# Key columns projected from rows without the shift, shift matmuls inside the first projection pass, and softmax read from PSUM, in an adaLN attention block on one core

## The chip, the cores and the metric

The kernel runs on one core of one Trainium2 chip. The metric is device time in microseconds of one execution. Executions are repeated, and each run is listed with its span in the trace and its mean granted TensorE clock. A run is put down as slow when it is over 1.5% above the fastest run of the same kernel; otherwise it is fast. Times of spans, windows and chains below are from the start of the traced span, which is some 1.8 us shorter than the measured time. In the views PE is TensorE, PEld its weight loads, DVE VectorE, ACT ScalarE and SPq the queue that issues transfers; psbank is a PSUM bank, PEclk the granted clock in tenths of full speed, and x with a number counts instructions. A "chain" is the work that ended last, followed back step by step to what released it.

## The reference

Shortened:

```python
B, N, D = (2, 256, 1152)          # bf16 everywhere
mod = (silu(c) @ w_mod).reshape(B, 6, 1, D)
shift_a, scale_a, gate_a, _, _, _ = [mod[:, i] for i in range(6)]
h   = layernorm(x) * (1 + scale_a) + shift_a
q, k, v = split(h @ wqkv)
p = softmax(einsum('bqd,bkd->bqk', q, k) * D ** -0.5)
return x + gate_a * (einsum('bqk,bkd->bqd', p, v) @ wo)
```

One fact of the arithmetic carries the change. If the key columns are made from h without the shift, every key of a batch element lacks the same vector (shift times the key weights). Its product with a query is the same number for all keys, so the softmax over keys cancels it. Queries and values still need the shift.

## The kernel before

All rows are 128-partition tiles: four token tiles, nine feature chunks. A small helper records operations in program order, and each engine is given its own in that order, with semaphore waits for dependences. The parts that matter, shortened:

```python
GROUPS = [(0, 2), (2, 5), (5, 7), (7, 9)]            # feature chunks modulated together
PASSES = [list(range(0, 7)), list(range(7, 14)), list(range(14, 18))]   # q,k column blocks
PASS1_BANKS = [5, 6, 0, 1, 2, 3, 4]
...
def warm(n):                                          # matmuls of zeros that keep TensorE busy
    for _ in range(n):
        op(PE, lambda pe: pe.matmul(ps[7][:, 0:512], warm_sb[:, 0:P], warm_sb[:, 0:512], ...))
...
xT(0); warm(3); xT(1); warm(2)                        # transposes of normalised rows
mod_mm(0, 1); xT_out(0, ...); mod_mm(0, 0); mod_ev(0) # scale and shift of group 0
...
for g, (a, b_) in enumerate(GROUPS):                  # pass 0, in four groups
    if g > 0:
        mod_mm(g, 1); mod_mm(g, 0)                    # scale and shift of this group
        mod_ev(g)                                     # PSUM -> SBUF on DVE
        for cc in range(a, b_):
            for b in range(B):
                modulate(cc, b, ...)                  # hT = xnT * scale + shift
    for k in range(a, b_):
        for j, bank in zip(PASSES[0], PASS1_BANKS):
            qk_mm(0, j, k, bank)
for n, (j, bank) in enumerate(zip(PASSES[0], PASS1_BANKS)):
    evac(DVE if n % 2 == 0 else AC, qkT_sb[:, j, :], ps[bank][:, 0:T], ...)
...                                                   # passes 1 and 2, then v, scores, softmax
```

Softmax copies the scores from PSUM to SBUF on ACT, takes scaled values and their maximum on DVE, then does the exponential on ACT. The weights arrive on one queue, modulation columns and first-pass rows alternating by group.

Of the kernel before, what the change touches and what calls it, by code (L numbers as in the profile page):

```python
# [153 lines left out]
GROUPS = [(0, 2), (2, 5), (5, 7), (7, 9)]  # L154
PASSES = [list(range(0, 7)), list(range(7, 14)), list(range(14, 18))]
# [17 lines left out]
def _build(nc, es, x, c, wqkv, wo, w_mod, out):  # L173
# [19 lines left out]
    s_sb = sb("s_sb", [P, TT, NTOK], bf16)  # L193
# [34 lines left out]
    wm_off = {}  # L228
    off = 0
    for g, (a, b_) in enumerate(GROUPS):  # L230
        for kind in range(2):
            wm_off[(g, kind)] = off
            off += DC * (b_ - a) * P

    def wm_ap(g, kind):
        w = (GROUPS[g][1] - GROUPS[g][0]) * P
        return bass.AP(wm_sb, wm_off[(g, kind)], [[2 * DC * D, P], [w, DC], [1, w]])
# [3 lines left out]

    def wm_keys(lo, hi):
        keys = []
        for (g, kind), o in wm_off.items():
            n = DC * (GROUPS[g][1] - GROUPS[g][0]) * P
            if o < hi and o + n > lo:
                keys.append(("wm", g, kind))
        return keys
# [6 lines left out]
    def dma_mod(g):  # L255
        a, b_ = GROUPS[g]
        for kind in (1, 0):
            base = kind * D
            op(SP, lambda e, g=g, kind=kind, lo=base + a * P, hi=base + b_ * P:
               e.dma_start(wm_ap(g, kind), wm_v[:, :, lo:hi]), w=[("wm", g, kind)], dma=True)  # L260

    def dma_wq(k0, k1, c0, c1, keys):
        op(SP, lambda e: e.dma_start(wq_sb[:, k0:k1, c0:c1], wq_v[:, k0:k1, c0:c1]),
           w=keys, dma=True)

    def wkeys(p, k0, k1):
        return [("w", p, k) for k in range(k0, k1)]

    for g, (a, b_) in enumerate(GROUPS):
        dma_mod(g)  # L270
        dma_wq(a, b_, 0, 7 * P, wkeys(0, a, b_))
    for k0 in range(0, DC, 3):
        dma_wq(k0, k0 + 3, 7 * P, 14 * P, wkeys(1, k0, k0 + 3))
    for k0 in range(0, DC, 3):
        dma_wq(k0, k0 + 3, 14 * P, 18 * P, wkeys(2, k0, k0 + 3))
    for k0 in range(0, DC, 3):
        dma_wq(k0, k0 + 3, 2 * D, 3 * D, wkeys(3, k0, k0 + 3))
# [17 lines left out]
    def warm(n):  # L295
        for _ in range(n):
            op(PE, lambda pe: pe.matmul(ps[7][:, 0:512], warm_sb[:, 0:P], warm_sb[:, 0:512],  # L297
                                        start=True, stop=True),
               r=[("warm",)], w=[("ps", 7)])
# [5 lines left out]
    def f_cT(pe):  # L305
        last = None
        for k in range(DC):
            last = pe.transpose(psb[6][:, 2 * k:2 * k + 2], c_sb[0:2, k * P:(k + 1) * P],
                                ident[0:2, 0:2])
        return last  # L310
    op(PE, f_cT, r=[("c",), ("ident",)], w=[("ps", 6)])
    cT_ps = psb[6][:, 0:2 * DC].rearrange("p (k b) -> p k b", b=2)
    op(DVE, lambda v: v.tensor_copy(cT_sb[:, :, :], cT_ps), r=[("ps", 6)], w=[("cT",)])
    op(AC, lambda a: a.activation(e1_sb[:, :, :], cT_sb[:, :, :], ACT.Exp, scale=-1.0),
       r=[("cT",)], w=[("e1",)])
    warm(8)

# [68 lines left out]
    def mod_mm(g, kind):  # L386
        a, b_ = GROUPS[g]
        w = (b_ - a) * P
        for cc in range(a, b_):
            col = (kind * DC + cc) * 2  # L390
            for k in range(DC):
                op(PE, lambda pe, cc=cc, k=k, col=col, src=wm_ap(g, kind), lo=(cc - a) * P: pe.matmul(  # L392
                    ps[7][:, col:col + 2], src[:, k, lo:lo + P], scT_sb[:, k, 0:2],
                    start=(k == 0), stop=(k == DC - 1)),
                   r=[("wm", g, kind), ("scT",)], w=[("ps", 7)])
# [3 lines left out]
    def mod_ev(g):  # L399
        a, b_ = GROUPS[g]  # L400
        op(DVE, lambda v: v.tensor_scalar(mod_sb[:, 1, a:b_, :], mod_ps[:, 1, a:b_, :], 1.0, None,  # L401
                                          op0=ALU.add), r=[("ps", 7)], w=[("sc", g)])
        op(DVE, lambda v: v.tensor_copy(mod_sb[:, 0, a:b_, :], mod_ps[:, 0, a:b_, :]),  # L403
           r=[("ps", 7)], w=[("sh", g)])

    group_of = {cc: g for g, (a, b_) in enumerate(GROUPS) for cc in range(a, b_)}

    def modulate(cc, b, eng):
        g = group_of[cc]
        dst = hT_sb[:, cc, b * NTOK:(b + 1) * NTOK]  # L410
        src = xnT_sb[:, cc, b * NTOK:(b + 1) * NTOK]
        sc, sh = mod_sb[:, 1, cc, b:b + 1], mod_sb[:, 0, cc, b:b + 1]
        rk, wk = [("xnT", cc, b), ("sc", g), ("sh", g)], [("hT", cc, b)]
        if eng == DVE:
            op(DVE, lambda v: v.tensor_scalar(dst, src, sc, sh, op0=ALU.mult, op1=ALU.add), r=rk, w=wk)  # L415
        else:
            op(AC, lambda a: a.activation(dst, src, ACT.Identity, bias=sh, scale=sc), r=rk, w=wk)  # L417

    stats_dve(0)
# [6 lines left out]
    rstd(0)  # L426
    sq_act(1)
    stats_dve(2)
    stats_act_end(1)
    xn(0)  # L430
    rstd(1)
    rstd(2)
    xn(1)
    xn(2)
    sum_act(3)
    sq_act(3)
    xT(0)
    warm(3)
    xT(1)
    warm(2)  # L440
    mod_mm(0, 1)
    xT_out(0, lambda bank: DVE)
    mod_mm(0, 0)
    mod_ev(0)
    modulate(0, 0, DVE)
    modulate(1, 0, DVE)
    stats_act_end(3)
    rstd(3)
    xn(3)
    xT(2)  # L450
    xT(3)
    xT_out(1, lambda bank: DVE if bank % 2 == 0 else AC)
    modulate(0, 1, DVE)
# [216 lines left out]
```

## Time and profile before

| | before |
|---|---|
| median of the first three runs | 112.39 us (111.78 to 112.62) |
| span of the profiled run | 110.1 us |
| TensorE busy | 99.1 us, 90% |
| first matmul of pass 0 | 16.19 us |
| pass 0, first to last of 63 matmuls | 23.9 us |
| one undisturbed 512-column matmul | 0.219 us |

The prediction shows the slices and the chain. One more view is worth knowing, the table of waits (engine, what it was to make, what it waited for: us in total, times, longest). TensorE's own waits for other engines' work in pass 0 are one line of it:

```profile
PE psbank L459 <- DVE hT_sb L415: 3.5, 4, 1.0
```

These are the four group starts: the projection (L459) waits for the modulated rows (L415). The three inside pass 0 make 2.9 us.

### The profile page before, as it was taken

To read this page: it belongs to the slowest core of one execution; us is meant where nothing else is said; L and a number is where in the kernel's file an instruction comes from. 1 tells how busy PE (TensorE), PEld (TensorE's weight loads), DVE (VectorE), ACT (ScalarE), POOL (GpSimd) and SP (SyncE) were. 2 spreads that over 40 slices of the span, in tenths; PEclk is the share of its full clock that TensorE was granted. 3 is DMA by queue.
4 is the path that set the end of the run, shared out by engine and by line. 5 is a ranking of instruction groups with operands and counts; after the bars stand their busy time and mean duration, and the time that the engine had idled before them with its cause. 6 is when DMAs were issued, how large, how long until landed. Compare 5 with 4: busy or idle time off the path is not lost.

```text
span 110.1 us, 1775 instructions
## 1 busy us (share of the span) xinstructions
PE 99.1 (90%) x735; PEld 56.2 (51%) x735; DVE 43.9 (40%) x125; ACT 26.7 (24%) x61; POOL 4.2 (4%) x17
## 2 busy tenths in 40 slices
PE   5959459969969699999999999999999999999990
PEld 1407333533445334444444568766666875655570
DVE  0798570040030380000800422643422785666672
ACT  4579230030020250000500415461111870000000
POOL 6610000000000000000000000000000000000000
PEclk9999955785999999999999999999999999999999
DMA  3999999999999999996299400000000001112222
GB/s 77 323 309 321 333 332 348 292 329 294 369 382 363 366 390 389 396 392 232 20 361 408 176 0 0 6 3 0 0 0 0 6 0 33 56 54 70 71 77 71
DMA packets 18956, 21.06 MB, mean 191 GB/s; under 512 B 770, under 2 KB 14978, under 8 KB 18948
## 3 DMA queue, kind: packets, MB, share of 16 engines
q1 hardware_dynamic: 18944, 20.94, 58.7%
q8 instruction: 6, 0.10, 0.4%
q14 instruction: 2, 0.02, 0.1%
q10 hardware_dynamic: 4, 0.00, 0.0%
HBM read 19.76 MB, written 1.18 MB: 190 GB/s over the span
## 4 chain that ended last, share of the span: by engine, by line
PE 81%; DMA 7%; DVE 6%; SPq 2%; issue 1%; ACT 0%
PE psbank L459 36%; PE psbank L509 16%; PE psbank L620 16%; DMA wm_sb<-in_w_mod_dram 7%; PE psbank L585 4%; PE psbank L522 4%; PE psbank L392 3%; DVE hT_sb L415 2%; SPq L253 2%; PE psbank L572 1%; DVE xnT_sb L381 1%; PE psbank L601 1%; DVE mod_sb L401 1%; DVE ga_sb L627 1%; DVE xo_sb L362 1%
## 5 line engine op out<-in xcount | busy, mean ns | idle before, releaser
L459 PE MATMUL psbank<-hT_sb,wq_sb 128*128 128x512 bf16 x162 | 39.6, 408 | 3.5 <-DVE hT_sb L415 3.5
L459 PEld LDWEIGHTS psbank<-hT_sb,wq_sb 128*128 128x128 bf16 x162 | 16.3, 104 | 25.4 <-issue 5.1
L509 PE MATMUL psbank<-wq_sb,hT_sb 128*128 128x384 bf16 x108 | 18.0, 326 | 0.0
L620 PE MATMUL psbank<-wm_sb,pvT_sb 128*128 128x384 bf16 (+2 forms) x117 | 17.7, 314 | 0.0
L620 PEld LDWEIGHTS psbank<-wm_sb,pvT_sb 128*128 128x128 bf16 x117 | 11.1, 98 | 6.6
L509 PEld LDWEIGHTS psbank<-wq_sb,hT_sb 128*128 128x128 bf16 x108 | 10.5, 98 | 6.9
L466 DVE CAST qkT_sb<-psbank 128x512 bf16<-128x512 f32 x10 | 6.3, 684 | 18.9 <-PE psbank L459 18.9
L468 ACT ACTIVATE qkT_sb<-psbank 128x512 bf16<-128x512 f32 x8 | 4.2, 597 | 21.2 <-PE psbank L459 21.2
L627 DVE TENSOR_TENSOR ga_sb<-psbank,gate_rep 128x384 bf16<-128x384 f32 (+2 forms) x13 | 6.8, 526 | 5.9 <-PE psbank L620 5.9
L297 PE MATMUL psbank<-warm_sb 128*128 128x512 bf16 x17 | 6.9, 556 | 1.2 <-DVE warm_sb L280 1.2
L401 DVE TENSOR_SCALAR mod_sb<-psbank 128x4 f32<-128x4 f32 (+1 forms) x4 | 0.7, 164 | 17.7 <-PE psbank L392 17.7
L417 ACT ACTIVATE hT_sb<-xnT_sb,mod_sb 128x256 bf16<-128x256 bf16 x4 | 2.3, 596 | 18.6 <-DVE mod_sb L403 18.6
L466 DVE CAST v_sb<-psbank 128x384 bf16<-128x384 f32 x6 | 3.2, 555 | 7.7 <-PE psbank L509 7.7
L369 PE MATMUL psbank<-ident,xo_sb 128*128 128x128 bf16 x36 | 3.1, 242 | 3.4 <-DVE xo_sb L362 3.4
L468 ACT ACTIVATE v_sb<-psbank 128x384 bf16<-128x384 f32 x6 | 2.9, 486 | 10.3 <-PE psbank L509 10.3
L392 PEld LDWEIGHTS psbank<-scT_sb,wm_sb 128*128 128x128 bf16 x162 | 4.7, 96 | 1.3 <-DMA wm_sb<-in_w_mod_dram 0.3
L392 PE MATMUL psbank<-scT_sb,wm_sb 128*128 128x2 bf16 x162 | 4.8, 164 | 0.2 <-DMA wm_sb<-in_w_mod_dram 0.2
L369 PEld LDWEIGHTS psbank<-ident,xo_sb 128*128 128x128 bf16 x36 | 2.5, 108 | 4.7 <-DVE xo_sb L362 4.5
L630 DVE TENSOR_TENSOR xo_sb<-x_sb,ga_sb 128x384 bf16<-128x384 bf16 (+2 forms) x13 | 4.5, 342 | 0.4
L585 PE MATMUL psbank<-pT_sb,v_sb 128*128 128x256 bf16 x36 | 4.3, 273 | 0.0
L522 PE MATMUL psbank<-qkT_sb 128*128 128x256 bf16 x36 | 4.1, 273 | 0.0
L415 DVE TENSOR_SCALAR hT_sb<-xnT_sb,mod_sb 128x256 bf16<-128x256 bf16 x14 | 4.0, 342 | 0.1
(57 smaller groups left out, 59.0 us busy)
## 6 DMA issues: line engine op xcount, KB each, us to landing
wm_sb<-in_w_mod_dram SPq DMA_DIRECT2D x6, 576.0 KB, 8.3
wq_sb<-in_wqkv_dram SPq DMA_DIRECT2D x4, 672.0 KB, 8.6
wq_sb<-in_wqkv_dram SPq DMA_DIRECT2D x3, 864.0 KB, 11.1
wm_sb<-in_w_mod_dram SPq DMA_DIRECT2D x1, 2592.0 KB, 17.8
wm_sb<-in_wo_dram SPq DMA_DIRECT2D x1, 2592.0 KB, 9.2
wm_sb<-in_w_mod_dram SPq DMA_DIRECT2D x2, 864.0 KB, 8.9
wq_sb<-in_wqkv_dram SPq DMA_DIRECT2D x3, 448.0 KB, 8.3
x_sb<-in_x_dram SPq DMA_DIRECT2D x4, 288.0 KB, 3.6
```

What stands on the lines that cost most here:

```text
L297: op(PE, lambda pe: pe.matmul(ps[7][:, 0:512], warm_sb[:, 0:P], warm_sb[:, 0:512], start=True, stop=True), r=[("warm",)], w=[("ps", 7)])
L369: op(PE, lambda pe, cc=cc, bank=bank, half=half: pe.transpose(psb[bank][:, half * T + i * P: half * T + (i + 1) * P], xo_sb[:, i, cc * P:( ...
L392: op(PE, lambda pe, cc=cc, k=k, col=col, src=wm_ap(g, kind), lo=(cc - a) * P: pe.matmul(ps[7][:, col:col + 2], src[:, k, lo:lo + P], scT_s ...
L415: op(DVE, lambda v: v.tensor_scalar(dst, src, sc, sh, op0=ALU.mult, op1=ALU.add), r=rk, w=wk)
L459: op(PE, lambda pe: pe.matmul(ps[bank][:, lo:hi], wq_sb[:, k, j * P:(j + 1) * P], hT_sb[:, k, lo:hi], start=(k == 0), stop=(k == DC - 1)), ...
L466: op(DVE, lambda v: v.tensor_copy(dst, src), r=r, w=w)
L468: op(AC, lambda a: a.activation(dst, src, ACT.Copy), r=r, w=w)
L509: op(PE, lambda pe, k=k, q=q, bank=bank: pe.matmul(ps[bank][:, 0:384], hT_sb[:, k, i * P:(i + 1) * P], wq_sb[:, k, 2 * D + q * 384:2 * D + ...
L522: op(PE, lambda pe, cc=cc: pe.matmul(ps[bank][:, 0:NTOK], qkT_sb[:, cc, i * P:(i + 1) * P], qkT_sb[:, DC + cc, b * NTOK:(b + 1) * NTOK], s ...
L585: op(PE, lambda pe, h=h, cc=cc, sbk=sbk: pe.matmul(ps[bank][:, h * NTOK:(h + 1) * NTOK], v_sb[:, 2 * b + sbk, cc * P:(cc + 1) * P], pT_sb[ ...
L620: op(PE, lambda pe, i=i, k=k, c0=c0, c1=c1, n=n, bank=bank: pe.matmul(ps[bank][:, 0:n], pvT_sb[:, k, i * P:(i + 1) * P], wo_ap[:, k, c0:c1 ...
L627: op(DVE, lambda v, b=b, c0=c0, c1=c1, n=n, bank=bank, s=s: v.tensor_tensor(ga_sb[:, s, 0:n], ps[bank][:, 0:n], gate_rep[:, b, c0:c1], ALU ...
```

## The change

The intent is to take everything that TensorE waits for out of pass 0. The columns are reordered so that pass 0 makes key columns alone (blocks 11 to 17), from rows that are only scaled. The scale half of the modulation is made before pass 0, row by row as it arrives. The shift half is made by matmuls between those of pass 0, added to the rows after it, and used by passes 1 and 2 and by v. Weights come in longer rows. Softmax reads its scores from PSUM. The activation table set is not changed by the diff, and both profiles have one table load, of 1.28 us. The diff also reorders the row statistics on ACT and shares the evictions of the transposes between DVE and ACT in another way. No run takes these two, or the longer rows, out on their own.

```diff
-PASSES = [list(range(0, 7)), list(range(7, 14)), list(range(14, 18))]
+PASSES = [list(range(11, 18)), list(range(4, 11)), list(range(0, 4))]
@@ loads
-    for g, (a, b_) in enumerate(GROUPS):
-        dma_mod(g)
-        dma_wq(a, b_, 0, 7 * P, wkeys(0, a, b_))
+    for k0 in range(0, DC, 3):
+        dma_mod(1, k0, k0 + 3)                 # scale half, whole rows
+    dma_pass(0, [0, 1, 3, 6, 9])
+    for k0 in range(0, DC, 3):
+        dma_mod(0, k0, k0 + 3)                 # shift half
@@ before pass 0 (cut; the first burst of warm-ups goes from 8 to 6)
     xT(0)
-    warm(3)
+    for k in range(0, 3):
+        mod_mm(1, k)
+    warm(2)
     xT(1)
     warm(2)
...
     xT(2)
+    for k in range(3, 6):
+        mod_mm(1, k)
+    warm(3)
     xT(3)
     xT_out(1, ...)
+    warm(2)
+    for k in range(6, 9):
+        mod_mm(1, k)
+    op(DVE, ...)                               # 1 + scale, then scale(cc, b) for all rows
@@ pass 0
-    for g, (a, b_) in enumerate(GROUPS):
-        ...                                    # as shown above
+    for k in range(DC):
+        for j, bank in zip(PASSES[0], PASS1_BANKS):
+            qk_mm(0, j, k, bank)
+        if 5 <= k <= 7:
+            for kk in range(3 * (k - 5), 3 * (k - 4)):
+                mod_mm(0, kk)
+    op(DVE, lambda v: v.tensor_copy(mod_sb[:, 0, :, :], mod_ps[:, 0, :, :]), ...)
+    for cc in range(DC - 1):
+        for b in range(B):
+            shift(cc, b, DVE if (2 * cc + b) % 3 else AC)
     for n, (j, bank) in enumerate(zip(PASSES[0], PASS1_BANKS)):
         evac(DVE if n % 2 == 0 else AC, qkT_sb[:, j, :], ps[bank][:, 0:T], ...)
+    for b in range(B):
+        shift(DC - 1, b, DVE)
@@ softmax (cut)
-        op(AC, lambda a: a.activation(s_sb[:, i, :], ps[bank][:, 0:NTOK], ACT.Copy), ...)
-        op(DVE, ... s_sb * CONST_B, max into mx_sb ...)
+        op(DVE, lambda v: v.tensor_reduce(mx_sb[:, i:i + 1], ps[bank][:, 0:NTOK], AX.X, ALU.max), ...)
```

More of the change, by code (lines that the diff above doesn't have):

```diff
@@ L152 @@
 CONST_B = 0.0294189453125
-GROUPS = [(0, 2), (2, 5), (5, 7), (7, 9)]
-PASSES = [list(range(0, 7)), list(range(7, 14)), list(range(14, 18))]
+PASSES = [list(range(11, 18)), list(range(4, 11)), list(range(0, 4))]
 PASS1_BANKS = [5, 6, 0, 1, 2, 3, 4]
@@ L192, in _build @@
     wm_sb = sb("wm_sb", [P, 2 * DC * D], bf16)
-    s_sb = sb("s_sb", [P, TT, NTOK], bf16)
     e_sb = sb("e_sb", [P, TT, NTOK], bf16)
@@ L226, in _build, with wm_ap @@
     op = pg.op
-    wm_off = {}
-    off = 0
-    for g, (a, b_) in enumerate(GROUPS):
-        for kind in range(2):
-            wm_off[(g, kind)] = off
-            off += DC * (b_ - a) * P
-    def wm_ap(g, kind):
-        w = (GROUPS[g][1] - GROUPS[g][0]) * P
-        return bass.AP(wm_sb, wm_off[(g, kind)], [[2 * DC * D, P], [w, DC], [1, w]])
+    def wm_ap(kind):
+        return bass.AP(wm_sb, kind * DC * D, [[2 * DC * D, P], [D, DC], [1, D]])
     wgate_ap = bass.AP(wm_sb, 0, [[2 * DC * D, P], [D, DC], [1, D]])
     wo_ap = bass.AP(wm_sb, DC * D, [[2 * DC * D, P], [D, DC], [1, D]])
-    def wm_keys(lo, hi):
-        keys = []
-        for (g, kind), o in wm_off.items():
-            n = DC * (GROUPS[g][1] - GROUPS[g][0]) * P
-            if o < hi and o + n > lo:
-                keys.append(("wm", g, kind))
-        return keys
     op(AC, lambda e: e.dma_start(c_sb[:, :], c[:, :]), w=[("c",)], dma=True)
@@ L253, in _build, with dma_mod, dma_wq, dma_pass @@
         op(SP, lambda e, i=i: e.dma_start(x_sb[:, i, :], x_pi[:, i, :]), w=[("x", i)], dma=True)
-    def dma_mod(g):
-        a, b_ = GROUPS[g]
-        for kind in (1, 0):
-            base = kind * D
-            op(SP, lambda e, g=g, kind=kind, lo=base + a * P, hi=base + b_ * P:
-               e.dma_start(wm_ap(g, kind), wm_v[:, :, lo:hi]), w=[("wm", g, kind)], dma=True)
-    def dma_wq(k0, k1, c0, c1, keys):
-        op(SP, lambda e: e.dma_start(wq_sb[:, k0:k1, c0:c1], wq_v[:, k0:k1, c0:c1]),
-           w=keys, dma=True)
-    def wkeys(p, k0, k1):
-        return [("w", p, k) for k in range(k0, k1)]
-    for g, (a, b_) in enumerate(GROUPS):
-        dma_mod(g)
-        dma_wq(a, b_, 0, 7 * P, wkeys(0, a, b_))
+    def dma_mod(kind, k0, k1):
+        op(SP, lambda e: e.dma_start(wm_ap(kind)[:, k0:k1, :], wm_v[:, k0:k1, kind * D:(kind + 1) * D]),
+           w=[("wm", kind, k) for k in range(k0, k1)], dma=True)
+    def dma_wq(p, k0, k1, c0, c1):
+        op(SP, lambda e: e.dma_start(wq_sb[:, k0:k1, c0:c1], wq_v[:, k0:k1, c0:c1]),
+           w=[("w", p, k) for k in range(k0, k1)], dma=True)
+    def dma_pass(p, cuts):
+        c0, c1 = PASSES[p][0] * P, (PASSES[p][-1] + 1) * P
+        for k0, k1 in zip(cuts, cuts[1:]):
+            dma_wq(p, k0, k1, c0, c1)
     for k0 in range(0, DC, 3):
-        dma_wq(k0, k0 + 3, 7 * P, 14 * P, wkeys(1, k0, k0 + 3))
+        dma_mod(1, k0, k0 + 3)
+    dma_pass(0, [0, 1, 3, 6, 9])
     for k0 in range(0, DC, 3):
-        dma_wq(k0, k0 + 3, 14 * P, 18 * P, wkeys(2, k0, k0 + 3))
+        dma_mod(0, k0, k0 + 3)
+    dma_pass(1, [0, 3, 6, 9])
+    dma_pass(2, [0, 3, 6, 9])
     for k0 in range(0, DC, 3):
-        dma_wq(k0, k0 + 3, 2 * D, 3 * D, wkeys(3, k0, k0 + 3))
+        dma_wq(3, k0, k0 + 3, 2 * D, 3 * D)
     op(DVE, lambda v: v.memset(warm_sb[:, :], 0.0), w=[("warm",)])
@@ L296, in warm @@
         for _ in range(n):
-            op(PE, lambda pe: pe.matmul(ps[7][:, 0:512], warm_sb[:, 0:P], warm_sb[:, 0:512],
+            op(PE, lambda pe: pe.matmul(ps[6][:, 0:512], warm_sb[:, 0:P], warm_sb[:, 0:512],
                                         start=True, stop=True),
-               r=[("warm",)], w=[("ps", 7)])
+               r=[("warm",)], w=[("ps", 6)])
     op(AC, lambda a: a.preload_act_table_set("natural_log_exp_and_others"))
@@ L307, in f_cT @@
         for k in range(DC):
-            last = pe.transpose(psb[6][:, 2 * k:2 * k + 2], c_sb[0:2, k * P:(k + 1) * P],
+            last = pe.transpose(psb[5][:, 2 * k:2 * k + 2], c_sb[0:2, k * P:(k + 1) * P],
                                 ident[0:2, 0:2])
         return last
-    op(PE, f_cT, r=[("c",), ("ident",)], w=[("ps", 6)])
-    cT_ps = psb[6][:, 0:2 * DC].rearrange("p (k b) -> p k b", b=2)
-    op(DVE, lambda v: v.tensor_copy(cT_sb[:, :, :], cT_ps), r=[("ps", 6)], w=[("cT",)])
+    op(PE, f_cT, r=[("c",), ("ident",)], w=[("ps", 5)])
+    cT_ps = psb[5][:, 0:2 * DC].rearrange("p (k b) -> p k b", b=2)
+    op(DVE, lambda v: v.tensor_copy(cT_sb[:, :, :], cT_ps), r=[("ps", 5)], w=[("cT",)])
     op(AC, lambda a: a.activation(e1_sb[:, :, :], cT_sb[:, :, :], ACT.Exp, scale=-1.0),
        r=[("cT",)], w=[("e1",)])
-    warm(8)
     def stats_dve(i):
@@ L384, in xT_out, with mod_mm @@
                    r=[("ps", bank)], w=keys)
-    def mod_mm(g, kind):
-        a, b_ = GROUPS[g]
-        w = (b_ - a) * P
-        for cc in range(a, b_):
+    def mod_mm(kind, k):
+        for cc in range(DC):
             col = (kind * DC + cc) * 2
-            for k in range(DC):
-                op(PE, lambda pe, cc=cc, k=k, col=col, src=wm_ap(g, kind), lo=(cc - a) * P: pe.matmul(
-                    ps[7][:, col:col + 2], src[:, k, lo:lo + P], scT_sb[:, k, 0:2],
-                    start=(k == 0), stop=(k == DC - 1)),
-                   r=[("wm", g, kind), ("scT",)], w=[("ps", 7)])
@@ L397, in _build @@
-    mod_ps = ps[7][:, 0:4 * DC].rearrange("p (q c b) -> p q c b", q=2, b=2)
-    def mod_ev(g):
-        a, b_ = GROUPS[g]
-        op(DVE, lambda v: v.tensor_scalar(mod_sb[:, 1, a:b_, :], mod_ps[:, 1, a:b_, :], 1.0, None,
-                                          op0=ALU.add), r=[("ps", 7)], w=[("sc", g)])
-        op(DVE, lambda v: v.tensor_copy(mod_sb[:, 0, a:b_, :], mod_ps[:, 0, a:b_, :]),
-           r=[("ps", 7)], w=[("sh", g)])
-    group_of = {cc: g for g, (a, b_) in enumerate(GROUPS) for cc in range(a, b_)}
@@ L408, in modulate, with scale @@
-    def modulate(cc, b, eng):
-        g = group_of[cc]
+            op(PE, lambda pe, cc=cc, col=col: pe.matmul(
+                ps[7][:, col:col + 2], wm_ap(kind)[:, k, cc * P:(cc + 1) * P], scT_sb[:, k, 0:2],
+                start=(k == 0 and cc == 0), stop=(k == DC - 1), skip_group_check=True),
+               r=[("wm", kind, k), ("scT",)], w=[("ps", 7)])
+    mod_ps = ps[7][:, 0:4 * DC].rearrange("p (q c b) -> p q c b", q=2, b=2)
+    def scale(cc, b, eng):
         dst = hT_sb[:, cc, b * NTOK:(b + 1) * NTOK]
@@ L411, in modulate @@
         src = xnT_sb[:, cc, b * NTOK:(b + 1) * NTOK]
-        sc, sh = mod_sb[:, 1, cc, b:b + 1], mod_sb[:, 0, cc, b:b + 1]
-        rk, wk = [("xnT", cc, b), ("sc", g), ("sh", g)], [("hT", cc, b)]
+        sc = mod_sb[:, 1, cc, b:b + 1]
+        rk, wk = [("xnT", cc, b), ("sc",)], [("hT", cc, b)]
         if eng == DVE:
-            op(DVE, lambda v: v.tensor_scalar(dst, src, sc, sh, op0=ALU.mult, op1=ALU.add), r=rk, w=wk)
+            op(DVE, lambda v: v.tensor_scalar(dst, src, sc, None, op0=ALU.mult), r=rk, w=wk)
@@ L416, in modulate, with shift @@
         else:
-            op(AC, lambda a: a.activation(dst, src, ACT.Identity, bias=sh, scale=sc), r=rk, w=wk)
+            op(AC, lambda a: a.activation(dst, src, ACT.Copy, scale=sc), r=rk, w=wk)
+    def shift(cc, b, eng):
+        dst = hT_sb[:, cc, b * NTOK:(b + 1) * NTOK]
+        sh = mod_sb[:, 0, cc, b:b + 1]
+        rk, wk = [("hT", cc, b), ("sh",)], [("hT", cc, b)]
+        if eng == DVE:
+            op(DVE, lambda v: v.tensor_scalar(dst, dst, sh, None, op0=ALU.add), r=rk, w=wk)
+        else:
+            op(AC, lambda a: a.activation(dst, dst, ACT.Identity, bias=sh, scale=1.0), r=rk, w=wk)
@@ L419, in _build @@
+    warm(6)
     stats_dve(0)
@@ L425, in _build @@
     sum_act(1)
-    rstd(0)
     sq_act(1)
     stats_dve(2)
+    rstd(0)
     stats_act_end(1)
+    sum_act(3)
+    rstd(1)
     xn(0)
-    rstd(1)
+    sq_act(3)
     rstd(2)
     xn(1)
-    xn(2)
-    sum_act(3)
-    sq_act(3)
     xT(0)
-    warm(3)
+    for k in range(0, 3):
+        mod_mm(1, k)
+    warm(2)
     xT(1)
     warm(2)
-    mod_mm(0, 1)
-    xT_out(0, lambda bank: DVE)
-    mod_mm(0, 0)
-    mod_ev(0)
-    modulate(0, 0, DVE)
-    modulate(1, 0, DVE)
+    xT_out(0, lambda bank: DVE if bank < 3 else AC)
     stats_act_end(3)
+    xn(2)
     rstd(3)
@@ L450, in _build @@
     xT(2)
+    for k in range(3, 6):
+        mod_mm(1, k)
+    warm(3)
     xT(3)
-    xT_out(1, lambda bank: DVE if bank % 2 == 0 else AC)
-    modulate(0, 1, DVE)
-    modulate(1, 1, DVE)
+    xT_out(1, lambda bank: DVE if bank < 3 else AC)
+    warm(2)
+    for k in range(6, 9):
+        mod_mm(1, k)
+    op(DVE, lambda v: v.tensor_scalar(mod_sb[:, 1, :, :], mod_ps[:, 1, :, :], 1.0, None, op0=ALU.add),
+       r=[("ps", 7)], w=[("sc",)])
+    for cc in range(DC):
+        scale(cc, 0, DVE)
+        scale(cc, 1, DVE if cc % 2 == 0 else AC)
     def qk_mm(p, j, k, bank, b=None):
@@ L468, in evac @@
             op(AC, lambda a: a.activation(dst, src, ACT.Copy), r=r, w=w)
-    for g, (a, b_) in enumerate(GROUPS):
-        if g > 0:
-            mod_mm(g, 1)
-            mod_mm(g, 0)
-            mod_ev(g)
-            for cc in range(a, b_):
-                for b in range(B):
-                    modulate(cc, b, DVE if (cc + b) % 2 == 0 or cc == a else AC)
-        for k in range(a, b_):
-            for j, bank in zip(PASSES[0], PASS1_BANKS):
-                qk_mm(0, j, k, bank)
+    for k in range(DC):
[4 more added lines that the diff above has]
+                mod_mm(0, kk)
+    op(DVE, lambda v: v.tensor_copy(mod_sb[:, 0, :, :], mod_ps[:, 0, :, :]), r=[("ps", 7)], w=[("sh",)])
+    for cc in range(DC - 1):
+        for b in range(B):
+            shift(cc, b, DVE if (2 * cc + b) % 3 else AC)
     for n, (j, bank) in enumerate(zip(PASSES[0], PASS1_BANKS)):
         evac(DVE if n % 2 == 0 else AC, qkT_sb[:, j, :], ps[bank][:, 0:T], [("ps", bank)], [("qk", j)])
+    for b in range(B):
+        shift(DC - 1, b, DVE)
     for p in (1, 2):
@@ L489, in _build @@
             evac(DVE if n % 2 == 0 else AC, qkT_sb[:, j, :], ps[bank][:, 0:T], [("ps", bank)], [("qk", j)])
-    op(SP, lambda e: e.dma_start(wgate_ap, wm_v[:, :, 2 * D:3 * D]), w=[("wgate",)] + wm_keys(0, DC * D), dma=True)
-    op(SP, lambda e: e.dma_start(wo_ap, wo_v), w=[("wo",)] + wm_keys(DC * D, 2 * DC * D), dma=True)
+    op(SP, lambda e: e.dma_start(wgate_ap, wm_v[:, :, 2 * D:3 * D]), w=[("wgate",)] + [("wm", 0, k) for k in range(DC)], dma=True)
+    op(SP, lambda e: e.dma_start(wo_ap, wo_v), w=[("wo",)] + [("wm", 1, k) for k in range(DC)], dma=True)
     rot = [0]
@@ L529, in softmax @@
     def softmax(i, bank):
-        op(AC, lambda a: a.activation(s_sb[:, i, :], ps[bank][:, 0:NTOK], ACT.Copy),
-           r=[("ps", bank)], w=[("s", i)])
-        op(DVE, lambda v: v.tensor_scalar(s_sb[:, i, :], s_sb[:, i, :], CONST_B, None,
-                                          op0=ALU.mult, op1=ALU.max, accum_out=mx_sb[:, i:i + 1]),
-           r=[("s", i)], w=[("s", i), ("mx", i)])
-        op(DVE, lambda v: v.tensor_scalar(nb_sb[:, i:i + 1], mx_sb[:, i:i + 1], -1.0, None, op0=ALU.mult),
+        op(DVE, lambda v: v.tensor_reduce(mx_sb[:, i:i + 1], ps[bank][:, 0:NTOK], AX.X, ALU.max),
+           r=[("ps", bank)], w=[("mx", i)])
+        op(DVE, lambda v: v.tensor_scalar(nb_sb[:, i:i + 1], mx_sb[:, i:i + 1], -CONST_B, None, op0=ALU.mult),
            r=[("mx", i)], w=[("nb", i)])
-        op(AC, lambda a: a.activation(e_sb[:, i, :], s_sb[:, i, :], ACT.Exp, bias=nb_sb[:, i:i + 1],
-                                      scale=1.0, accum_out=rsum_sb[:, i:i + 1]),
-           r=[("s", i), ("nb", i)], w=[("e", i), ("rsum", i)])
+        op(AC, lambda a: a.activation(e_sb[:, i, :], ps[bank][:, 0:NTOK], ACT.Exp, bias=nb_sb[:, i:i + 1],
+                                      scale=CONST_B, accum_out=rsum_sb[:, i:i + 1]),
+           r=[("ps", bank), ("nb", i)], w=[("e", i), ("rsum", i)])
         op(DVE, lambda v: v.reciprocal(rinv_sb[:, i:i + 1], rsum_sb[:, i:i + 1]),
```

## The prediction

Three things in it are the author's estimates, shown by no trace: 0.45 us for a shift add on ACT, 0.5 us of clock lost on average by the hole before pass 1, and when the clock comes back in each of the three cases. The 596 ns are one ACT modulate of the kernel before, 128x256 with a scale and a bias (L417).

> **What bounds the kernel now.** I read the page's slices first, then the chain that ended last, then its pieces in order of time, then one-microsecond windows for the clock. The slices of 2.75 us each:
>
> ```profile
> PE   5959459969969699999999999999999999999990
> PEclk9999955785999999999999999999999999999999
> GB/s 77 323 309 321 333 332 348 292 329 294 369 382 363 366 390 389 396 392 232 20 361 408 176 0 0 6 3 0 0 0 0 6 0 33 56 54 70 71 77 71
> PE 81%; DMA 7%; DVE 6%; SPq 2%; issue 1%; ACT 0%
> ```
>
> TensorE is full from slice 15 (41 us) to the end, at full clock, and it is 81% of the chain. So whatever happens to softmax, evictions or output after 41 us costs nothing unless TensorE waits for it. What can be won lies before 41 us, where PE has holes and PEclk reads 5 to 8. The chain in order of time shows the holes:
>
> ```profile
> 3.06 8.22 DMA wm_sb<-in_w_mod_dram
> ...
> 16.19 5.29 PE psbank L459 x14
> 21.47 1.34 PE psbank L392 x54
> ...
> 23.11 0.61 DVE hT_sb L415 x2
> 23.72 0.05 issue
> 23.77 6.39 PE psbank L459 x21
> 30.16 0.89 PE psbank L392 x36
> ...
> 32.00 3.19 PE psbank L459 x14
> 35.20 0.89 PE psbank L392 x36
> ...
> 37.04 24.73 PE psbank L459 x113
> ```
>
> L459 is the q/k projection, L392 the modulation (w_mod times silu(c)). The last piece gives the undisturbed rate: 24.73/113 = 0.219 us per matmul. Pass 0 has 63 matmuls: 49 in the first three pieces and 14 in the fourth, so it ends at 37.04 + 14 x 0.219 = 40.1. It began at 16.19, so it takes 23.9 us for 13.8 us of work. The rest: 126 modulation matmuls 3.1 us (1.34+0.89+0.89); three waits for eviction and modulate 2.9 us (22.81 to 23.77, 31.05 to 32.00, 36.09 to 37.04); and slow matmuls, 14 at 0.378 and 21 at 0.304 us, 2.2 + 1.8 = 4.0 us. The windows show the clock behind the last item:
>
> ```profile
> 12.00:13.00 1.00, 0.46 (x9) 0.28 (x6) 0.93 (x6) 0.00 (x0) 0.00 (x0) 1.00 1.09 328
> 13.00:14.00 1.00, 0.00 (x0) 0.00 (x0) 0.40 (x2) 0.50 (x2) 0.00 (x0) 0.81 1.10 326
> ...
> 20.00:21.00 1.00, 1.00 (x5) 0.46 (x4) 0.00 (x0) 0.00 (x0) 0.00 (x0) 0.77 1.19 290
> ...
> 23.00:24.00 1.00, 0.23 (x1) 0.11 (x2) 0.96 (x6) 0.89 (x2) 0.00 (x0) 0.93 1.12 337
> 24.00:25.00 1.00, 1.00 (x4) 0.33 (x3) 0.22 (x1) 0.20 (x1) 0.00 (x0) 0.50 1.17 303
> ```
>
> The third number from the end is the clock. It halves at about 13.6 us, comes back at 20.46, halves again at 23.86 and comes back at 27.28.
>
> [...]here the early mix with 512-byte rows moved 291 to 353 GB/s and the 1,792-byte rows after 40 us 380 to 403. [...]with two (scale and bias) it took 596 ns here[...].
>
> **The change, part by part.**
>
> *Modulation in pass 0.* All nine scale rows are now made before pass 0 and all nine shift rows run inside it, after k = 5, 6 and 7, where nothing waits for them. Removed from pass 0: the three waits, -2.9 us. Its 126 modulation matmuls become 81 at 0.025 us (1.34/54): 2.0, so -1.1 us. The clock should be lost less in a pass without holes: the second cold stretch (1.8 us) goes.
>
> *Start of pass 0.* Now it waits for x and all of the scale half, 1.18 + 2.65 MB, where before 1.18 + 1.18 MB had to be in. With about 1.0 MB moved by 5 us and 0.39 MB/us for longer rows, and some 0.5 MB of others' data ahead (before, the 2.36 MB needed at 11.28 us landed when 2.9 had moved), the three scale pieces land at about 9.0, 11.3 and 13.5 us. That is not quite the bound; PE's own order is. From ACT's order (two 1.25 us passes over x for tile 1, one for tile 3, then the small ones) xn(1) ends near 9.9 and xn(3) near 13.7. PE then does, after xT(1): two warm-ups, xT(2) at 13.1, 27 modulations, three warm-ups, xT(3), two warm-ups, 27 modulations. At full clock this is 0.55+0.7+0.65+0.5+0.45+0.7 = 3.6, so 16.7; then the +1 eviction 0.2 and two scales 0.6: pass 0 starts at 17.5, +1.3 us. Half clock nearly doubles those terms (nine transposes took 1.14 us cold against 0.66): 1.0+0.9+1.3+1.0+0.85+0.9 = 5.9, so 19.0 and a start at 19.85, +3.7 us.
>
> *The shift after pass 0.* This is the new cost. It can start only when the last shift matmul is done (T0), while k = 8's seven matmuls (1.53 us) still run. DVE: eviction of the shift 0.2, ten adds at 0.26 (four modulates took 1.11 us), then the first q/k eviction 0.63: T0 + 3.4. ACT: six adds at about 0.45, then its evictions at 0.53. In engine order all seven bank evictions stand behind the adds, and pass 1 uses the same seven banks. Its k = 0 matmuls go at 3.45, 3.7, 4.05, 4.3, 4.7, 4.9 and 5.3, ending at T0 + 5.5 instead of 3.06. New hole: **+2.5 us**, on the path[...]. Before, the same boundary cost nothing: the 113 matmuls ran through at 0.219.
>
> *Scales.* 14 on DVE (0.26) and 4 on ACT; each k needs two and has 1.53 us of matmul. Hidden.
>
> *Softmax from PSUM.* Removes four ACT copies (0.37 us) and shortens the chain, but the p transposes start at 78.7 us and the last softmax scaling ended at 74.4. Hidden, 0. Later weights: about 8.6 MB must be in for the shift rows, by some 26 us; used after 27. Hidden. The tables stay the same set: one load before, one after.
>
> *Sum.* Steady part: -2.9 -1.1 +2.5 +0.5 = -1.0 us. Start and clock decide the rest. If the clock comes back by about 13.6[...]: start +1.3, all 4.0 us of clock loss gone: -3.7. If it comes back at about 17: start near 19.0, +2.8, clock loss about 0.3: -1.0 +2.8 -3.7 = -1.9. If it is cold at the start: +3.7, clock loss about 1.9: -1.0 +3.7 -2.1 = +0.6.
>
> **The rivals.**
> (1) *The warm-up decides.* All gain is eaten by a PE that is half-clocked from 10 us on and whose chain of transposes, warm-ups and modulations sets the start. For: from 5.9 to 10.1 PE has only nine transposes[...]. Against: the warm-up counts were changed in the diff, which looks tuned. Time about 112 to 113.
> (2) *The boundary hole is hidden or smaller*, because shift adds finish faster, 1 us of it: about 108 with a warm start. Against: both engines are loaded evenly, 2.6 us each by the rows above.
> (3) *DMA becomes the start's bound*: scale rows land after 15.6 us. At 0.33 MB/us the last lands near 15.1, so it costs little.
> (4) *A full win*: warm start[...]: 107.9.
>
> **Range and chances.** The median is 112.39 and the profiled run 111.99, so I count from the median[...]. Outcomes with weights 0.45, 0.3 and 0.25: 108.5, 110.3 and 112.8, mean 110.1; I shade it to 109.6, since a tuned warm-up makes the first likelier. Two per cent is 110.15. The range is 107.6 to 112.4. Faster 0.6, same 0.36, slower 0.04.
>
> **What would show it.** In the profile after: pass 0's first matmul at 17.5 (right) or near 20 (rival 1), with PEclk before it; pass 0 without waits, its 63 matmuls and 81 modulations in some 16 us; a PE gap of about 2 us before pass 1, released by the q/k eviction, with ten shift adds in front of it on DVE; everything after pass 1 unchanged in length; no wait before the p transposes. I am wrong if PE waits for weights in pass 0 or 1, if the gap before pass 1 is under 1 us or above 4[...].

## The result and the profile after

The changed kernel took 109.1 us in the median of 4 runs (107.15 to 111.48), against 112.5 of 4 runs before (111.78 to 113.04). The ratio is 0.958, with a 95% interval of 0.945 to 0.971. Ratios here are the mean time of one kernel's fast runs over that of the other's of the same rounds, so not quite the ratio of the medians. It is faster by more than 2%, and the median lies 0.5 us below the predicted 109.6.

The page of the first profile after. Its run took 109.89 us and is one of the two slow ones of the four:

```profile
PE   5916989799999499999999999999999999999990
PEclk9995555999999999999999999999999999999999
GB/s 92 313 292 401 398 384 381 390 393 382 380 363 362 391 393 392 390 393 393 381 76 0 0 0 3 6 0 0 0 0 0 6 0 36 73 61 48 79 73 73
PE 83%; DVE 8%; DMA 4%; issue 1%; SPq 1%
```

Slices are 2.7 us here. From slice 8 on (counted from 0, 21.6 us) TensorE has full clock and one visible hole, the 4 at 35 to 38 us. The half-clocked stretch (5555, from 8.6 to 18.8 us) has moved ahead of pass 0. DMA moves 360 to 400 GB/s from 8 us on, where before it moved 290 to 350 until 27 us.

A second profile of the same kernel, from the first experiment, fell in a fast run (107.56 us). It is the one to hold against the profile before, which was fast as well. Its chain, in order of time (start, length, what):

```profile
18.16 2.33 PE psbank L444 x10
20.49 0.05 issue
20.54 6.85 PE psbank L444 x31
27.40 0.65 PE psbank L371 x27
...
30.24 1.53 PE psbank L444 x7
31.77 0.67 PE psbank L371 x27
...
32.68 2.05 DVE hT_sb L393 x10
34.73 0.61 DVE qkT_sb L451
35.34 0.05 issue
35.39 9.95 PE psbank L444 x43
```

L444 is the projection, L371 the modulation, L393 the shift adds, L451 an eviction. Pass 0 now runs without a wait and at full rate. Three blocks of 27 shift matmuls stand in it at 0.65 to 0.67 us each. Then the chain leaves TensorE: ten shift adds and one eviction come before the first matmul of pass 1.

The two fast profiles, cut at the same events (a piece's matmuls are counted by their starts at 0.219 us; the last seven matmuls of pass 0 end at 33.83):

| part | before | after | difference |
|---|---|---|---|
| start of pass 0 | 16.19 | 18.16 | +1.97 |
| pass 0 | 23.91 | 15.67 | -8.24 |
| hole before pass 1 | 0 | 1.56 | +1.56 |
| passes 1 and 2, 99 matmuls | 21.67 | 22.04 | +0.37 |
| the rest | 48.33 | 48.37 | +0.04 |
| span | 110.1 | 105.8 | -4.3 |

So one part wins 8.2 us and gives back half: 2.0 at a later start and 1.9 at the boundary (the 0.37 in pass 1 belongs to it, as its first matmuls wait for bank after bank).

### The profile page after: what moved, and what is told of

It is laid out like the page before. It is cut to its first block, busy times and chain, and to the rows that moved or that the text cites. A ratio compares the mean times of both kernels' runs of the same rounds, so it can differ in the third digit from the quotient of the medians.

```text
span 108.0 us, 1771 instructions
## 1 busy us (share of the span) xinstructions
PE 97.4 (90%) x730; PEld 57.2 (53%) x737; DVE 44.2 (41%) x125; ACT 27.9 (26%) x65; POOL 4.3 (4%) x17
## 4 chain that ended last, share of the span: by engine, by line
PE 83%; DVE 8%; DMA 4%; issue 1%; SPq 1%
PE psbank L444 32%; PE psbank L497 16%; PE psbank L605 16%; DMA x_sb<-in_x_dram 4%; PE psbank L349 4%; PE psbank L371 4%; PE psbank L570 4%; PE psbank L510 4%; PE psbank L279 2%; DVE hT_sb L393 2%; DVE stat_sb L301 1%; PE psbank L557 1%; DVE xo_sb L342 1%; PE psbank L586 1%; SPq L236 1%
## 5 line engine op out<-in xcount | busy, mean ns | idle before, releaser
L444 PE MATMUL psbank<-hT_sb,wq_sb 128*128 128x512 bf16 x157 | 35.7, 379 | 2.5 <-DVE qkT_sb L451 1.4
L444 PEld LDWEIGHTS psbank<-hT_sb,wq_sb 128*128 128x128 bf16 x162 | 15.5, 98 | 21.2 <-DVE qkT_sb L451 2.8
L451 DVE CAST qkT_sb<-psbank 128x512 bf16<-128x512 f32 x10 | 6.3, 685 | 16.8 <-PE psbank L444 16.8
L279 PE MATMUL psbank<-warm_sb 128*128 128x512 bf16 x17 | 8.2, 603 | 1.7 <-DVE warm_sb L262 1.2
L453 ACT ACTIVATE qkT_sb<-psbank 128x512 bf16<-128x512 f32 x8 | 4.2, 590 | 18.8 <-PE psbank L444 18.8
L349 PE MATMUL psbank<-ident,xo_sb 128*128 128x128 bf16 x36 | 4.6, 313 | 3.8 <-DVE xo_sb L342 3.8
L349 PEld LDWEIGHTS psbank<-ident,xo_sb 128*128 128x128 bf16 x36 | 3.9, 146 | 6.3 <-DVE xo_sb L342 5.2
L451 DVE CAST v_sb<-psbank 128x384 bf16<-128x384 f32 x6 | 3.3, 557 | 8.2 <-PE psbank L497 8.2
L395 ACT ACTIVATE hT_sb<-hT_sb,mod_sb 128x256 bf16<-128x256 bf16 x6 | 2.5, 496 | 13.3 <-DVE mod_sb L463 13.3
L371 PEld LDWEIGHTS psbank<-scT_sb,wm_sb 128*128 128x128 bf16 x162 | 5.2, 100 | 1.3 <-issue 0.6
L371 PE MATMUL psbank<-scT_sb,wm_sb 128*128 128x2 bf16 x162 | 5.1, 165 | 0.0
L361 DVE COPY xnT_sb<-psbank 128x512 bf16<-128x512 bf16 x6 | 2.2, 418 | 5.1 <-PE psbank L349 5.1
## 6 DMA issues: line engine op xcount, KB each, us to landing
wq_sb<-in_wqkv_dram SPq DMA_DIRECT2D x5, 672.0 KB, 13.6
```

What stands on the lines that cost most here:

```text
L279: op(PE, lambda pe: pe.matmul(ps[6][:, 0:512], warm_sb[:, 0:P], warm_sb[:, 0:512], start=True, stop=True), r=[("warm",)], w=[("ps", 6)])
L349: op(PE, lambda pe, cc=cc, bank=bank, half=half: pe.transpose(psb[bank][:, half * T + i * P: half * T + (i + 1) * P], xo_sb[:, i, cc * P:( ...
L371: op(PE, lambda pe, cc=cc, col=col: pe.matmul(ps[7][:, col:col + 2], wm_ap(kind)[:, k, cc * P:(cc + 1) * P], scT_sb[:, k, 0:2], start=(k = ...
L444: op(PE, lambda pe: pe.matmul(ps[bank][:, lo:hi], wq_sb[:, k, j * P:(j + 1) * P], hT_sb[:, k, lo:hi], start=(k == 0), stop=(k == DC - 1)), ...
L451: op(DVE, lambda v: v.tensor_copy(dst, src), r=r, w=w)
L453: op(AC, lambda a: a.activation(dst, src, ACT.Copy), r=r, w=w)
```

## The experiments

All kernels gave correct results. Each had six runs, beside eleven runs of the kernel before in each of the three batches, each batch on one chip; the fast runs of before averaged 111.61, 111.55 and 111.44 us. The third batch ran on another chip than the first two. Some comparisons below cross batches; the means of before, 0.2 us apart, say how much that can matter. The changed kernel's runs are in the first batch. The cut between fast and slow goes through a spread here, so a kernel with many slow runs is flattered by the mean of its fast ones; where that matters, the length from start to end decides. "Start to end" is the time from pass 0's first matmul to the end of the span. It separates what happens before pass 0 from what happens after.

### The changed kernel again

No edit.

> The changed kernel unchanged, for more executions and a second profile. Theory (clock of the prologue): times again spread over some 3 to 4 us (107 to 111.5), and a profile of a shorter run has the clock back earlier than 18.84 us and pass 0's first matmul earlier than 20.41 us; the stretch from that matmul to the end differs by under 1 us. Rival (the spread arises later, by the hole before pass 1 costing the clock): pass 0 starts at 20.4 in all, and the difference lies after 34 us.

Measured: 107.33 to 108.30 us, all six fast, ratio 0.966. The expected spread did not show up in this batch. What the second profile says holds all the same: start at 18.16 instead of 20.41, and start to end 87.64 against 87.59. The two profiles differ before pass 0 and nowhere else. In the slow profile the chain before pass 0 ends so:

```profile
14.01 1.14 PE psbank L349 x9
15.15 0.70 PE psbank L371 x27
...
17.15 0.96 PE psbank L349 x9
18.11 0.85 PE psbank L279 x2
18.96 0.67 PE psbank L371 x27
```

In the fast one, the same pieces:

```profile
13.64 0.82 PE psbank L349 x9
14.46 0.65 PE psbank L371 x27
...
15.78 0.50 PE psbank L349 x9
16.29 0.43 PE psbank L279 x2
16.72 0.67 PE psbank L371 x27
```

L349 are transposes, L279 warm-ups. A warm-up at half clock has 0.43 us from start to start, at full clock 0.22. In the slow run the clock came back at 18.8 us; in the fast one the full rate came back during the transposes that start at 13.64 (nine in 0.82 us, against 1.14 in the slow run, and the next nine in 0.50). One caution: the page of the fast run reads PEclk 9 in all 40 slices, although its warm-ups and transposes before 13.6 us ran at half rate. In that profile the clock reads 1.00 in every microsecond from 5 to 17 us, while two warm-ups from 12.18 us took 1.06 us. In the profile before it reads 1.00 up to 13.5 us, while the warm-ups from 3.33 us stood 0.43 us apart. The distance between starts of like matmuls is what shows the rate there.

### Eight more warm-ups

```diff
-    warm(6)
+    warm(14)
     stats_dve(0)
```

> Eight more warm-up matmuls (14 for 6) while TensorE waits for the first normalised rows. Theory: the clock, lost at 8.6 us in the profile after, is kept; transposes, warm-ups and modulations run at full rate, pass 0 starts near 17.5 us, not 20.4, and the time is 106 to 107 us with a spread under 1.5 us. Rival (data and the vector engines set the start): start within 0.5 us of 20.4, time as the changed kernel's.

Measured: 107.47 us median, fast runs 107.29 on average against 107.80 of the unchanged kernel in the same batch. Repeated in the third batch:

> The variant with 14 warm-ups again, on the same chip as the one before, for the comparison: 107.0 to 107.6 in fast runs, pass 0 from 17.7 us.

Measured: 107.28 median, fast runs 107.15 on average. Pass 0 starts at 17.70 and 17.77 in the two profiles, and start to end is 87.6 in both. The clock is kept (nine transposes of the third tile take 0.68 us, two warm-ups 0.43, in both profiles), so the start near 17.5 that the prediction gave for a full-rate prologue is right to 0.3 us. The time is above the 106 to 107 expected, the spread is 2.4 us where under 1.5 was expected, and one run in six was still slow each time (108.98 and 109.41). That is a gain of 0.5 us over a good run of the changed kernel, about the scatter of single runs, and 2.7 us in the start over its slow profile. More clock does not help further, as TensorE now waits: in both profiles it is idle for 1.17 us before the third tile's transposes (13.32 and 13.39 us), for rows that DVE normalises.

### No warm-ups after the first four

All of the calls after the first were taken out, 15 matmuls (the text on record miscounts them as 13):

```diff
-    warm(6)
...
-    warm(2)                                    # before xT(1)
-    warm(2)                                    # after xT(1)
...
-    warm(3)                                    # before xT(3)
-    warm(2)                                    # after xT(3)
```

> The changed kernel with only the first four warm-up matmuls (13 taken away). Theory: without them the clock is half until pass 0 itself brings it back; pass 0 starts near 18 us, no later than in a good run of the changed kernel because 7 slow warm-ups (3 us) are gone from TensorE's chain, but its first 7 to 14 matmuls take 0.43 us: 1 to 2.5 us slower than the changed kernel's fast runs, 108.8 to 110.3. Rival (warm-ups are only delay): faster than the changed kernel.

Measured: 109.25 us median, 109.31 mean, all runs fast; 1.5 us slower than the changed kernel's 107.80. Its chain:

```profile
17.60 11.17 PE psbank L439 x42
```

Pass 0 starts 0.56 us earlier than in the fast profile of the changed kernel, and its first 42 matmuls take 11.17 us where 42 x 0.219 = 9.2 would do: +2.0. Together +1.4, as measured. In this run nine transposes from 13.30 us took 1.14 us, where 0.68 was measured with 14 warm-ups. So warm-ups are not mere delay.

### The kernel before, with its clock kept

Eight warm-ups into bank 6, in TensorE's idle time before the last transposes. Nothing else.

```diff
     xT(2)
+    warm6(8)
     xT(3)
```

> The kernel before, with eight warm-up matmuls put into TensorE's idle time before the last transposes (12.4 to 14.4 us), and nothing else. Theory (a good part of the gain is the clock): pass 0's first matmuls run at 0.22 us instead of 0.378, its start stays at about 16.2 us, and the time falls by some 2 us (110 to 110.5). Rival (the gain of the change is the removed waits alone): within 0.5 us of before.

Measured: 110.76 us median; fast runs 109.64 on average against 111.55 of before, ratio 0.983 (0.973 to 0.993). All runs of both, whatever their state, average 110.44 and 112.41, 2.0 us apart, so the state of the runs does not make the difference. Its chain, from a run counted as slow:

```profile
17.23 3.19 PE psbank L467 x14
20.42 1.34 PE psbank L399 x54
...
22.72 6.39 PE psbank L467 x21
```

The first 14 matmuls take 3.19 us where they took 5.29. The second group is still slow at 6.39, as it was. The start came later than the 16.2 expected (17.23): the first transposes began at 8.73 us instead of 8.41, and the warm-ups, transposes and modulations from 9.5 to 13 us ran at half clock (nine transposes in 0.96 us, two warm-ups in 0.85). So about half of the clock loss in pass 0 (2.1 of 4.0 us) can be saved without any of the change. The 1.9 us between the fast runs is half of the 3.8 by which the changed kernel's beat before in the first batch.

### Shift adds of rows 0 to 3 before the evictions, the rest after

```diff
-    for cc in range(DC - 1):
+    for cc in range(4):
         for b in range(B):
             shift(cc, b, DVE if (2 * cc + b) % 3 else AC)
     ...                                        # the seven evictions
-    for b in range(B):
-        shift(DC - 1, b, DVE)
+    for cc in range(4, DC):
+        for b in range(B):
+            shift(cc, b, DVE if (2 * cc + b) % 3 else AC)
```

> Only the order of the shift adds: those of rows 0 to 3 before the seven evictions, the rest after. Theory: the hole before pass 1 (2.0 us of lost matmul time in the profile after) falls to about 0.9, so 1.1 us faster than the changed kernel of the same rounds at the same start of pass 0. Rival (the hole is hidden by later slack or set by something else): no change in the length from pass 0's start to the end.

Measured: fast runs 106.47 us on average against 107.80, so 1.3 faster. But three of the six were slow, against none of the changed kernel's, and the median of all six is 107.74, so this difference is not firm. What is firm is start to end, 86.65 against 87.64, or 1.0 us. Its chain at the boundary:

```profile
34.77 1.07 DVE hT_sb L393 x5
35.84 0.61 DVE qkT_sb L451
36.45 0.05 issue
36.50 9.95 PE psbank L444 x43
```

Five adds instead of ten stand before the eviction, and pass 1 starts 1.96 us after the shift matmuls end (34.54), where it was 2.95 (32.44 to 35.39). So 1.0 of the hole's 1.56 us came from the order of work on DVE and ACT; some 0.6 is left, before an eviction that still stands behind five adds.

### The softmax of before in the changed kernel

The softmax of before was put back, with its SBUF buffer.

> The changed kernel with the softmax of before (copy to memory first). Theory: off the path, time as the changed kernel's within 0.3 us apart from the clock's spread; from pass 0's first matmul to the end the same to 0.1 us. Rival (softmax from PSUM carries part of the gain): 0.5 us or more slower in the stretch between score matmuls and p transposes.

Measured: fast runs 107.43 us on average against 107.80, start to end 87.58 against 87.64. The means are 0.37 apart where 0.3 was expected, but two of the six runs were slow and the faster kernel is the one with the old softmax; the length from start to end agrees to 0.1 us. Reading from PSUM is worth nothing here. ACT's timeline says why. Before (start, busy, engine, line, operation, wait before it), two softmax tiles:

```profile
68.24 0.51 ACT L537 ACTIVATE e_sb<-s_sb,nb_sb 128x256 bf16<-128x256 bf16 x1 [0.68 <-DVE nb_sb L535]
69.92 0.51 ACT L537 ACTIVATE e_sb<-s_sb,nb_sb 128x256 bf16<-128x256 bf16 x1 [0.81 <-DVE nb_sb L535]
```

After, in the first profile:

```profile
65.73 0.47 ACT L522 ACTIVATE e_sb<-psbank,nb_sb 128x256 bf16<-128x256 f32 x1 [1.14 <-DVE nb_sb L520]
67.36 0.47 ACT L522 ACTIVATE e_sb<-psbank,nb_sb 128x256 bf16<-128x256 f32 x1 [1.07 <-DVE nb_sb L520]
```

One tile follows the other after 1.63 us instead of 1.68: most of the 0.36 us of the removed copy has become a longer wait for DVE (1.07 for 0.81), which goes through the four tiles in order. And the four tiles are done by 71.7 us, while the transposes of p start at 76.8.

### Scale and shift both before pass 0

The shift rows are loaded ahead of pass 0's weights, both halves are made before pass 0, and each row gets one operation with scale and shift. No shift matmuls in pass 0, no adds after it. With 14 warm-ups, and 4 and 4 more in the waits for the shift rows:

```diff
     dma_mod(1, ...)
+    dma_mod(0, ...)
     dma_pass(0, [0, 1, 3, 6, 9])
-    dma_mod(0, ...)
...
+    for kk in range(0, 3): mod_mm(0, kk)
+    warm(4)
+    for kk in range(3, 6): mod_mm(0, kk)
+    warm(4)
+    for kk in range(6, 9): mod_mm(0, kk)
...
-        scale(cc, b, ...)
+        modulate(cc, b, ...)                   # xnT * scale + shift
```

> The changed kernel with 14 warm-ups, but scale and shift both made and applied before pass 0, as one operation; shift rows are loaded ahead of pass 0's weights, and eight more warm-ups stand in that wait. No shift adds after pass 0, no shift matmuls in it. Theory: pass 0 starts when the shift rows are in, near 21.9 us instead of 17.7 (+4.2), but the stretch from there to the end is shorter by 2.0 (81 matmuls) and 2.0 (hole): total within 1 us of the variant with 14 warm-ups, so the reordered shift itself is worth little. Rival (taking the shift off the start is the heart of the gain): 3 us or more slower.

Measured: 111.0 us median, fast runs 110.70 on average, 3.4 above the variant with 14 warm-ups. The theory expected a total within 1 us and missed; by its number the rival (3 us or more) holds. Pass 0 starts at 24.11, later than the 21.9 expected:

```profile
4.93 15.09 DMA wm_sb<-in_w_mod_dram
20.02 0.05 issue
20.06 0.83 PE psbank L371 x27
20.89 1.55 PE psbank L279 x4
22.44 0.77 PE psbank L371 x27
```

TensorE waited for shift rows until 20.06, then spent 1.55 us on my own last four warm-ups, mostly at half clock (0.39 us each on average, where 0.43 is the half rate and 0.22 the full one). These cost little, as the last shift rows landed only at 22.27. But the first matmuls of pass 0 were slow as well (1.65 us over 157). That left two causes mixed, the rows and the clock, so the warm-ups were set anew, 10 and 5:

> As the variant with all modulation before pass 0, but with 10 and 5 warm-ups in the two waits for shift rows instead of 4 and 4, so that the clock is kept: there 157 matmuls from pass 0's start took 36.03 us, 1.65 more than at 0.219. Theory (the last shift rows land near 22.2 us, so loading them first is what costs): start still at about 23.8, no slow matmuls, 83.6 us from there to the end, 108.5 to 109.2, still 1 us or more above the variant with 14 warm-ups and the shift after pass 0. Rival (only the clock made it slow): equal to that variant.

Measured: fast runs 109.02 us on average (spans 106.8, 107.6, 107.3), against 107.15 of the variant with 14 warm-ups in the same batch: 1.9 slower. The median of all six is 110.13; three were slow, the profiled one among them:

```profile
19.95 2.18 PE psbank L279 x10
22.13 0.65 PE psbank L371 x27
22.78 1.10 PE psbank L279 x5
23.88 0.67 PE psbank L371 x27
...
25.45 34.66 PE psbank L464 x159
```

There pass 0 starts at 25.45, not the 23.8 expected, at full rate (34.66/159 = 0.218), and start to end is 83.65, as expected. In this slow run the late start is my own doing: the last shift rows had landed at 21.20, but TensorE stood behind 15 warm-ups and took them up at 23.88. If the length holds in the fast runs, their pass 0 started at 23.2 to 24.0; no fast run was profiled, so this is worked out and not seen. It is near what the rows allow: they landed at 21.20 and 22.27 in the two profiles, and some 1.6 us of matmuls and vector work follow. This answers what the reordered shift is worth: after pass 0 it costs 4 us (87.6 against 83.65, half of it the 81 matmuls, half the hole), before pass 0 it saves about 6, so 1.9 us net. How much of that better-placed warm-ups would win back was not tried.

### Combination

14 warm-ups; the first 27 scale matmuls after the transposes of tile 1 and not before; split shift adds; pass 1 begins in bank 7, which is free.

```diff
     xT(0)
-    for k in range(0, 3):
-        mod_mm(1, k)
     warm(2)
     xT(1)
-    warm(2)
+    for k in range(0, 3):
+        mod_mm(1, k)
+    warm(3)
...
-        banks = PASS1_BANKS if p == 1 else [7] + PASS1_BANKS[0:3]
+        banks = [7] + PASS1_BANKS[0:6] if p == 1 else [4, 7] + PASS1_BANKS[0:2]
```

(The bank order of the later parts was turned to match, and one burst of 3 warm-ups became 2.)

> Combination: 14 warm-ups; the scale matmuls of the first three row blocks after the second tile's transposes, not before; shift adds of rows 0 to 3 ahead of the evictions and the rest behind; pass 1 begins in the free bank 7. Theory: pass 0 starts near 15.5 to 16 us, hole under 0.5 us: from pass 0's first matmul to the end 86.1 us, time 103.5 to 104.5. Rival (DMA): scale rows land too late for a start before 17 us, time 105.

Measured: 104.73 us median (103.86 to 104.95), a little above the expected range, all six fast, ratio 0.938 (0.932 to 0.943).

```profile
16.67 9.24 PE psbank L444 x42
...
32.91 21.66 PE psbank L444 x98
```

Pass 0 starts at 16.67, where 15.5 to 16 was expected, without a slow matmul; the chain now runs over ACT's passes over x and its row statistics (5.99 to 10.89 us) and not over the scale rows, so the rival (DMA) is not what holds it. Start to end is 86.2, as expected. This beats the changed kernel by 3 us, and its runs lie within 1.1 us of each other.

## Why the prediction was right

The time was forecast as 109.6 and measured as 109.1, faster by over 2%, which had the largest chance. By its steps:

- **Where the time could come from.** Right. The table above has -8.24 us in pass 0 and +0.04 in all that follows pass 2. The working's three terms for pass 0 (waits 2.9, fewer modulation matmuls 1.1, clock 4.0) make 8.0.
- **Pass 0.** The working had 23.9 us before, and 13.8 + 2.0 = 15.8 after with no wait and full clock; measured 15.67. The modulation blocks took 0.65 to 0.67 us, as 27 x 0.025 gives. No wait for weights or shift rows occurred in any profile with the changed order.
- **Start of pass 0.** The mechanism was right: TensorE's own chain of transposes, warm-ups and modulations sets the start, and the clock sets the length of the chain (from the third tile's transposes to the last modulation 5.62 us in the slow profile, 3.75 in the fast one, 3.60 with 14 warm-ups). The three cases were 17.5, 19.0 and 19.85. Measured: 17.70 and 17.77 with the clock kept by more warm-ups, 18.16 when it came back at about 14, and 20.41 when it came back at 18.8. The changed kernel itself did not start at 17.5, as TensorE is at half clock for much of the prologue in both profiles. Against the nearest case the working was 0.7 us too early (17.5 for 18.16) and 0.6 (19.85, the cold case, for 20.41). The length of TensorE's chain at full clock was right (3.6 us given, 13.32 to 16.92 measured with 14 warm-ups); what was early is its begin, the third tile's transposes, given as 13.1 and measured at 13.32 to 14.01.
- **The hole before pass 1.** Right in kind, size too large: predicted 2.5, measured 1.56 + 0.37 = 1.9. The mis-sized term is the shift add on DVE. It was taken from modulates with two per-partition operands, 0.26 us from start to start; the adds with one took 2.05/10 = 0.205. (One modulate took 342 ns, one add 283.) ACT's six took 2.50 us, 0.42 each, where 0.45 was the author's estimate. (One modulate on ACT took 596 ns, one add 496.)
- **Clock lost by that hole, +0.5 on average.** The author's estimate, and not seen in any of the profiles with the hole: in the fast profile after, 49 matmuls of passes 1 and 2, from 45.39 us, took 10.74 us, 0.219 each. Whether it happens in some unprofiled run is open. One run of the split variant took 111.24 us and was not profiled; what slowed it is not known.
- **Softmax, tables.** Hidden, 0, as said and as the experiment shows.
- **The rivals.** The first (the warm-up decides, 112 to 113) does describe what makes a slow run, but not its size: the slow profile starts 2.25 us later than the fast one, about as the working has it, yet the clock was back before pass 0, so the further 1.9 us of slow matmuls in pass 0 did not come. Even the slow profile is 2.1 us shorter than the one before. The second (a smaller hole) is true by 0.6 us. The third (the last scale rows land after 15.6 us) did not happen: they landed at 14.2 and 14.4 in the two profiles, and TensorE did not wait for them. What the fast profile's chain passes is the first third of these rows, landed at 9.63. The fourth (a full win, 107.9) is what the fast runs are, 107.73 on average here and 107.80 in the six later ones, though with a later start and a shorter hole than it was added up from.
- **Two slips in the working.** The rows after 40 us before are the 2,304-byte rows of v; the 1,792-byte rows of the second pass had landed by 36 us. And 108.5, 110.3 and 112.8 are counted from 112.2, between the median and the profiled run, and not from the median. Nothing hangs on either.

The forecast total was helped by its mixture: it averaged starts that were too early with a hole that was too long. It was helped by luck too: two of the four runs were slow. In the next batch none of six was, and the median was 107.71, just inside the range. The direction and the mechanism do not rest on that draw; the agreement to 0.5 us does.

The causes, then. Shown by the traces: the waits inside pass 0 and the clock loss inside it are gone. Shown by experiment too: 2.0 us of the clock loss come back without the warm-ups, and about 2 us of it could have been saved in the kernel before; 1.0 us of the hole is an order of work; the softmax is neutral. Deferring the shift is worth 1.9 us between fast runs with the clock meant to be kept; the start behind that number was not seen. Open: why a run in six is still slow with 14 warm-ups. The mean granted clock of these two runs is 0.966; an estimate from that, with the clock taken as full or half as in the traces, is some 7 us at half clock, so the clock was lost in them too; where, no profile shows. Open as well: what the longer rows and the new order of row statistics do to the start.

## What to carry to other kernels

Before work is moved off the path, look at which engine's in-order queue it moves to and what stands behind it there: here sixteen small adds ahead of seven evictions turned into 1.9 us of idle TensorE, and putting half of them behind won back a microsecond for nothing. Warm-up matmuls between the small steps of the prologue were worth their time here: with the first four alone, the first 42 matmuls of pass 0 took 2.0 us more and the kernel 1.5 us more; with eight more, pass 0 started at 17.70 us instead of 18.16 or 20.41. Their effect is read from the distance between starts of like matmuls (0.43 us at half clock, 0.22 at full) and not from the clock row alone. Cutting the span at one fixed event, here the first projection matmul, makes run-to-run luck before it and real differences after it separable to 0.1 us.
